# S4 block with adaLN and a Mish MLP: input transform behind each chunk on TensorE, VectorE's small work dealt out, parameters of blocks 1 and 2 at the start

## The chip, the cores and the metric

One core of a Trainium2 chip runs the whole program in one launch. The metric is device time in microseconds, the median of three runs. Five engines work from queues of their own: TensorE (PE, its weight loads shown as PEld), VectorE (DVE), ScalarE (ACT), GpSimd (POOL) and SyncE (SP), which here issues nearly all DMAs.

## The reference

A sequence of 2048 rows of 512 features goes through a state-space convolution and a two-layer MLP, each behind a layer norm whose scale, shift and gate come from a conditioning vector:

```python
mod = (_silu(c) @ w_mod).reshape(1, 6, 1, -1)      # sa, ca, ga, sb, cb, gb
h = _layernorm(x) * (1 + ca) + sa
x = x + ga * ssm(h)                                # below
h = _layernorm(x) * (1 + cb) + sb
x = x + gb * (mish(h @ w1 + b1) @ w2)              # 512 -> 1792 -> 512

# ssm: each of 512 features has 128 complex states (A, B, C) and a step dt
P = exp(dt * A * arange(2048))                     # (512, 128, 2048)
K = sum_n(C_n * P_n * dt * B_n).real               # a filter of 2048 taps for each feature
y = irfft(rfft(K, 4096) * rfft(h, 4096))[:2048] + h * Dskip
```

All arrays are float32.

## The kernel before

It has three stages. The **generation stage** (to about 319 us) makes the filters `K` of all features and takes them, and the normalized input, through the first step of a Fourier transform. The **product stage** finishes both transforms, multiplies them and transforms back. The **dense stage** is the MLP. Only the first is touched.

*Blocks and chunks.* The 512 features are four blocks of 128; a block is eight chunks of 16 features, so there are 32 chunks, `k` = 0 to 31. A power P over 2048 steps is put together from a coarse and a fine part, so for each chunk:

- `s_ang` (TensorE): two groups of four matmuls turn the block's phases into angles, into `pang`. `s_sin` (ScalarE): absolute value and two sines of these into `ec`, three instructions. It runs two chunks ahead; `ec` has three buffers, and the one for chunk k + 2 is free when TensorE has read that of chunk k - 1.
- `coarse` (TensorE, then ScalarE): magnitudes by a matmul into `pco` and an Exp into `co`. This is made for a whole block in one go, the **visit** before the block's first chunk: 16 matmuls and 16 Exps through two PSUM buffers, between two ScalarE table loads (the Exp and the sine do not share a table).
- `s_mag` and `s_comb` (VectorE): `m` from `co` (one product of 1024 elements for each partition), then four products of `ec` with `m` and `co`, of 1024, 512, 512 and 1024. Before, `m` has one buffer and is made at the end of the chunk in front.
- `s_kgen` (TensorE): 32 small matmuls of `ec` with itself give the filter in `pkg`; `s_ks` (ScalarE) copies it to `ks`, `s_skip` (VectorE) adds the skip term, `s_ka` (TensorE) takes it through the first Fourier step into `pka`, and `s_tm` (ScalarE) copies that to `gk`.

*Parameters.* `params(b, stage)` turns a block's raw B, C and A into the numbers that the phases come from. Its 35 or so VectorE instructions of 128 or 256 elements for each partition are in stages 0, 2, 3 and 5; stage 1 (Ln and Exp) and stage 4 (Arctan) are ScalarE's. The result `pk` is stored to DRAM, and loaded back in another layout as `s` (the tiles s3 and s12). Before, block 0 is done at the start, stages 0 and 2 of block 1 too; the rest of blocks 1 to 3 is spread over chunks 1, 2, 4 and 5 of the blocks in front.

*Input.* The rows come in eight tiles `x` of two halves. `u_stats` (VectorE) makes mean and variance of two tiles, `u_norm` (VectorE, four instructions) normalizes a tile with the gains, `u_mm` (TensorE) takes a half through its first Fourier step into `pua`, and `u_out` (ScalarE and a DMA) copies and stores it. The gains need the modulation: `mod_mm` (TensorE), `mod_out` (ScalarE, and a store to `md`), and `gains` loads that row back.

*What sets the order.* In the generation stage nothing is left to the scheduler: each instruction of VectorE, ScalarE and TensorE is chained to the one recorded before it on its engine. The order is that of the loop at line 561, which puts together a list for each chunk: first what the table `pe` has (the input's matmuls), then `s_ka`, `s_kgen`, `s_ang`, then ScalarE's parts with what `se` has, then `s_comb`, `s_skip` and what `ve` has (normalization, statistics, parameters), then a visit where one is due, then `s_mag` of the next chunk:

```python
steps = pe.get(k, []) + [(s_ka, k - 3), (s_kgen, k - 1), (s_ang, k + 3)]
steps += [(s_tm, k - 3), (s_ks, k - 1)] + se.get(k, []) + [(s_sin, k + 2)]
steps += [(s_comb, k), (s_skip, k - 2)] + ve.get(k, [])
```

The visits have other work dealt into them, by the number of the Exp behind which it stands: both halves of an angle group, a filter, a Fourier step.

Of the kernel before, what the change touches and what calls it, by code (L numbers as in the profile page):

```python
# [10 lines left out]
F32 = mybir.dt.float32  # L11
# [5 lines left out]
OP = mybir.AluOpType  # L17
# [67 lines left out]
def s4_block(ctx, tc, io, out):  # L85
# [39 lines left out]
    V, A = Ordered(nc.vector, "dve"), Ordered(nc.scalar, "act")  # L125

# [93 lines left out]
    def params(b, stage):  # L220
        r = raw[b]
# [25 lines left out]
        if stage == 1:  # L247
            act(row[2], w2, AF.Ln)
            act(row[3], row[2], AF.Exp, scale=-0.5)
# [16 lines left out]
        if stage == 4:  # L266
            act(row[2], row[7], AF.Arctan)
# [10 lines left out]
        if stage == 5:  # L278
# [3 lines left out]
            split(0, 2 if b == 0 else 6)  # L282

    CO, S3 = {}, {}

    def load_s(b, eng):
        for h in range(2):
            eng.dma_start(S12[(2 * b + h) % 3][0:64].bitcast(F32),
                          view(pkd, (P * b + 64 * h) * 12 * P, [[3 * P, 64], [16 * 12 * P, 4], [1, 2 * P]]))

    def load_s3(b, eng):
        eng.dma_start(pkd[b], PKR[b].rearrange("p i e n -> p (i e n)").bitcast(F32))
        S3[b] = pre.tile([64, 8, P], F32R, tag="s3", name=f"s3_{b}")
        eng.dma_start(S3[b].bitcast(F32), view(pkd, P * b * 12 * P + 2 * P,
                                               [[3 * P, 64], [16 * 12 * P, 8], [1, P]]))
# [28 lines left out]
    def s_mag(k):  # L324
        m = M2[k] = gen.tile([P, 16, 64], F32, tag="m2", name=f"m2_{k}", bufs=1)
# [4 lines left out]
    def s_comb(k):  # L330
        ec, m = EC[k], M2[k]
        V.tensor_mul(ec[:, :, :, 32:64], ec[:, :, :, 95:63:-1], m[:, None, :, 0:32].to_broadcast([P, 2, 16, 32]))
        V.tensor_mul(ec[:, 0, :, 64:96], ec[:, 0, :, 64:96], m[:, :, 32:64])
        V.scalar_tensor_tensor(ec[:, 1, :, 64:96], ec[:, 1, :, 64:96], -1.0, m[:, :, 32:64],
                               op0=OP.mult, op1=OP.mult)
        V.tensor_mul(ec[:, :, :, 0:32], ec[:, :, :, 0:32], CO[k][:, None, :, 0:32].to_broadcast([P, 2, 16, 32]))
# [60 lines left out]
    def rsqrt(dst, var, n, pool, tag):  # L397
# [16 lines left out]
    def gains():  # L414
        g = conv.tile([P, 2, D], F32, name="gs")
# [5 lines left out]
        g12.append(g)  # L421

# [9 lines left out]
    def u_stats(n):  # L432
        s6 = conv.tile([P, 4, 6], F32, tag="bst", name="bst", bufs=2)
        for h in range(4):
            V.bn_stats(s6[:, h], XT[n + h // 2][:, h % 2])
            V.bn_aggr(mv[:, 2 * n + h, :], s6[:, h])
        rsqrt(rstd[:, 2 * n:2 * n + 4], mv[:, 2 * n:2 * n + 4, 1], 4, conv, "rsq")

    def u_norm(n):
        x = XT[n]  # L440
        for h in range(2):
            j = 2 * n + h
            V.scalar_tensor_tensor(x[:, h], x[:, h], mv[:, j, 0:1], g12[0][:, 1], op0=OP.subtract, op1=OP.mult)
# [379 lines left out]
```

## Time and profile before

| | us |
|---|---|
| median of 3 runs | 779.54 (778.78 to 780.31) |
| the profiled execution | 780.22 |
| its span | 778.4 |
| PE, DVE, ACT busy in the span | 667.6, 441.8, 316.0 |
| mean granted clock of PE | 0.898 of full speed |

The page divides the span in 40 slices of 19.5 us; each digit is a busy share in tenths (9 is 90% or more), PEclk the granted clock in tenths of 2.4 GHz:

```
PE   0498679866986899999993699999999999999996
DVE  8278998797879769487762922443244315242113
PEclk9959865896598779999995799999999999999999
```

The first 16 slices are the generation stage: there PE's clock is mixed and PE is busy for 4 to 9 tenths behind the first slice, VectorE for 2 to 9. From the 17th slice on PE is busy for nearly all of each slice at full clock, but for the change from the product to the dense stage at 410 to 439 us. A row of the trace gives, for each instruction or group, its start and duration, the engine, the line, the operation, what it writes and reads, and in brackets how long its engine was idle before it and whom it waited for.

### The profile page before, as it was taken

What the parts mean: (1) busy time and instruction counts of PE and PEld (TensorE: products, weight loads), DVE (VectorE), ACT (ScalarE), POOL (GpSimd) and SP (SyncE); (2) the same over time, 40 slices, a digit from 0 to 9 for tenths busy, and PEclk for the clock granted to TensorE, in tenths of its full rate; (3) what the DMA queues carried; (4) which work ended last, traced back from release to release, by engine and by line L of the source; (5) the groups of instructions that cost most, each with busy time, mean ns of one, the idle gap of its engine ahead of it and who ended that gap; (6) DMA issues with size and microseconds to landing.
All of it is one profiled execution on the core that took longest, in us unless ns stands there. A gap on an engine that the chain in (4) does not pass through costs nothing.

```text
span 778.4 us, 11803 instructions
## 1 busy us (share of the span) xinstructions
PE 667.6 (86%) x4848; PEld 448.3 (58%) x4848; DVE 441.8 (57%) x813; ACT 316.0 (41%) x466; POOL 5.0 (1%) x12
## 2 busy tenths in 40 slices
PE   0498679866986899999993699999999999999996
PEld 0256445543564565433330486888778877888885
DVE  8278998797879769487762922443244315242113
ACT  1456446664584686444430532232223221222220
POOL 2000000000000000000000000000000000000000
PEclk9959865896598779999995799999999999999999
DMA  6604201610151053799827652204220220002002
GB/s 183 228 1 144 80 31 56 210 56 28 55 164 55 29 189 110 207 287 294 281 98 182 194 123 55 54 1 109 54 55 1 47 62 1 0 7 49 0 1 54
DMA packets 34218, 74.56 MB, mean 96 GB/s; under 512 B 5322, under 2 KB 9806, under 8 KB 33652
## 3 DMA queue, kind: packets, MB, share of 16 engines
q1 hardware_dynamic: 33284, 72.17, 32.1%
q10 hardware_dynamic: 576, 1.05, 0.7%
q8 instruction: 38, 0.62, 0.3%
q0 software_dynamic: 304, 0.59, 0.3%
q14 instruction: 16, 0.13, 0.1%
HBM read 49.66 MB, written 24.13 MB: 95 GB/s over the span
## 4 chain that ended last, share of the span: by engine, by line
PE 74%; DVE 13%; ACT 6%; issue 3%; DMA 2%; SPq 0%; DVEq 0%; ACTq 0%
PE pm L712 20%; PE po L729 20%; PE pang L134 5%; PE pka L134 4%; PE pub L470 4%; PE pkg L134 4%; PE pz L632 4%; PE pkb L470 4%; DVE ec L119 3%; PE pco L134 3%; PE pua L134 3%; DVE raw L119 2%; PE pmod L134 2%; ACT ec L128 2%; PE pia L677 1%
## 5 line engine op out<-in xcount | busy, mean ns | idle before, releaser
L712 PE MATMUL pm<-hh,w1h 128*128 128x512 f32 x448 | 142.6, 398 | 0.6 <-ACT hh L119 0.6
L128 ACT ACTIVATE mh<-pm,b 128x512 f32<-128x512 f32 x56 | 38.5, 688 | 228.1 <-PE pm L712 228.1
L119 DVE TENSOR_TENSOR mal<-mh,mah 128x512 fp32r<-128x512 f32 x56 | 38.7, 691 | 155.3 <-ACT mah L119 154.9
L712 PEld LDWEIGHTS pm<-hh,w1h 128*128 128x128 f32 x448 | 84.7, 189 | 21.7 <-ACT hh L119 1.6
L729 PE MATMUL po<-w2h,mah 128*128 128x512 f32 x224 | 89.4, 399 | 0.0
L712 PE MATMUL pm<-hh,w1l 128*128 128x512 f32 x224 | 88.7, 396 | 0.0
L729 PE MATMUL po<-w2l,mah 128*128 128x512 f32 x224 | 88.6, 395 | 0.0
L729 PE MATMUL po<-w2h,mal 128*128 128x512 f32 x224 | 88.5, 395 | 0.0
L134 PE MATMUL pang<-ac,s 96*128 96x512 f32 x128 | 56.8, 482 | 26.6 <-DMA s<-pkd 26.6
L119 DVE TENSOR_TENSOR ec<-ec,m 128x1024 f32<-128x1024 f32 x64 | 61.3, 958 | 12.0 <-ACT ec L128 7.4
L134 PE MATMUL pua<-x,da 64*128 64x512 f32 x64 | 30.9, 946 | 30.2 <-DVE x L119 23.4
L134 PEld LDWEIGHTS pka<-bdk,ks 128*64 128x64 f32 x512 | 35.1, 166 | 31.8 <-issue 24.3
L119 DVE TENSOR_TENSOR m<-co 128x1024 f32<-128x1024 f32 x32 | 39.0, 1219 | 23.7 <-ACT co L128 23.7
L134 PE MATMUL pka<-bdk,ks 128*64 128x128 f32 x512 | 44.0, 327 | 7.9 <-DVE ks L119 7.9
L729 PEld LDWEIGHTS po<-w2h,mah 128*128 128x128 f32 x224 | 42.1, 188 | 14.6 <-ACT mah L119 4.9
L119 DVE TENSOR_TENSOR y<-pkb,f 128x1024 f32<-128x1024 f32 x32 | 37.7, 1219 | 22.6 <-PE pkb L470 16.7
L134 PEld LDWEIGHTS pang<-ac,s 96*128 96x128 f32 x128 | 28.2, 220 | 37.0 <-issue 30.6
L712 PEld LDWEIGHTS pm<-hh,w1l 128*128 128x128 f32 x224 | 42.4, 189 | 10.0
L729 PEld LDWEIGHTS po<-w2h,mal 128*128 128x128 f32 x224 | 42.1, 188 | 10.2
L729 PEld LDWEIGHTS po<-w2l,mah 128*128 128x128 f32 x224 | 42.1, 188 | 9.8
L134 PE MATMUL pco<-mc,s 64*128 64x384 f32 x64 | 32.4, 586 | 17.6 <-ACT co L128 17.6
L134 PE MATMUL pang<-am,s 96*128 96x512 f32 x128 | 44.8, 436 | 0.0
(96 smaller groups left out, 914.0 us busy)
## 6 DMA issues: line engine op xcount, KB each, us to landing
ud<-u SPq DMA_DIRECT2D x16, 512.0 KB, 2.9
ur<-ud SPq DMA_DIRECT2D x32, 256.0 KB, 5.2
zd<-z SPq DMA_DIRECT2D x16, 512.0 KB, 3.0
zl<-zd SPq DMA_DIRECT2D x28, 256.0 KB, 4.9
x<-in_A_u SPq DMA_DIRECT2D x32, 128.0 KB, 3.0
x<-in_A_u SPq DMA_DIRECT2D x8, 512.0 KB, 7.2
out<-ot SPq DMA_DIRECT2D x32, 128.0 KB, 2.4
w1s<-in_B_w SPq DMA_DIRECT2D x8, 448.0 KB, 6.4
```

The costliest lines, as they stand in the source:

```text
L119: ins = getattr(self.engine, name)(*a, **kw)
L128: follow("act", nc.scalar.activation(out, in_, f, **kw))
L134: follow("pe", T.matmul(out, lhsT, rhs, start=start, stop=stop))
L470: T.matmul(p[64 * r:64 * r + 64, c, :], MQ["mf", q // 4][:, 2 * (q % 4) + r, 64 * c:64 * c + 64], rhs(r), start=True, stop=True)
L632: T.matmul(p[:, r, :], mi[64 * r:64 * r + 64, q % 4, c, :], Y[q][64 * r:64 * r + 64, c, :], start=(c == 0), stop=(c == 1))
L677: T.matmul(p[64 * tl:64 * tl + 64, :], di, ZL[tt, hv][:, j % 2, tl, :], start=True, stop=True)
L712: T.matmul(p, w1[wi][:, k, fs], hh[:, hi, k, :], start=(n == 0), stop=(n == 3 * KB - 1))
L729: T.matmul(PO[tt][q], a[ai][:, P * q:P * q + P], w2[wi][:, f, :], start=(f == 0 and n == 0), stop=(f == FB - 1 and n == 2))
```

## The change

Five things change, all in the generation stage.

1. *Order on TensorE.* In a chunk the filter and the angles come first, then the Fourier step of the filter, and the input's matmuls (`u_mm`) last; their output copies (`u_out`) move one chunk later.
2. *Order on VectorE.* The small functions no longer issue their instructions; they return lists (class `Later`). The loop deals a chunk's small instructions out between the chunk's own large products. `m` of the next chunk stands behind the first product of `ec`, and has two buffers.
3. *Normalizations* are put at other chunks, three of them (table `vt`) at the end of chunks 7, 15 and 23, in front of a visit.
4. *Parameters.* Blocks 1 and 2 are computed together, instruction by instruction in turn, at the start, between block 0's and the first sines, and stored there; block 3's stay in the loop, at chunks 2, 5, 8 and 10.
5. *Visits* are bare: only the 16 matmuls and Exps (visit 0 has the products of chunk 0 and `m` of chunk 1 on VectorE). The angles of chunk 2 come after visit 0.

The core of the diff:

```diff
+    class Later:
+        def add(self, f, *a, **kw):
+            self.ops.append(lambda: f(*a, **kw))
+        def __getattr__(self, name):
+            return lambda *a, **kw: self.add(getattr(V, name), *a, **kw)
...
     def load_params(b):
-        raw[b] = gen.tile([P, 16, P], F32, tag="raw" if b else "ec", name=f"raw{b}", bufs=1 if b else 3)
-        (load if b < 2 else nc.sync.dma_start)(raw[b][:, 0:6, :], io["par"][b].rearrange("p (k n) -> p k n", k=6))
+        raw[b] = gen.tile([P, 16, P], F32, tag="raw" if b % 2 else "ec", name=f"raw{b}", bufs=1 if b % 2 else 3)
+        load(raw[b][:, 0:6, :], io["par"][b].rearrange("p (k n) -> p k n", k=6))
...
     def s_mag(k):
-        m = M2[k] = gen.tile([P, 16, 64], F32, tag="m2", name=f"m2_{k}", bufs=1)
+        m = M2[k] = gen.tile([P, 16, 64], F32, tag="m2", name=f"m2_{k}", bufs=2)
...
+    def run(*lists):
+        for i in range(max(map(len, lists))):
+            for ops in lists:
+                if i < len(ops):
+                    ops[i]()
...
+    store_pk(0)
+    load_s(0)
+    load_params(2)
...
-    params(1, 0)
+    V.on = A.on = True
+    run(params(1, 0), params(2, 0))
+    tables("natural_log_exp_and_others")
+    run(params(1, 1), params(2, 1))
+    tables("trig_and_small")
+    run(u_stats(0), params(1, 2), params(2, 2))
+    run(params(1, 3), params(2, 3))
+    run(params(1, 4), params(2, 4))
+    run(params(1, 5))
+    store_pk(1)
+    load_params(3)
...
-    visit(0, {2: [(s_mag, 0), (s_comb, 0), (s_ang, 2, 0)], 4: [(s_ang, 2, 1), (s_mag, 1)], 9: [(s_kgen, 0)]})
+    run(params(2, 5))
+    visit(0, {2: [lambda: step(s_mag, 0), lambda: run(comb(0))], 4: [lambda: step(s_mag, 1)]})
+    store_pk(2)
+    s_ang(2)
...
-    for n, k in enumerate((4, 6, 8, 10, 14, 16, 20, 24)):
+    for n, k, d in ((0, 4, ve), (1, 7, vt), (2, 9, ve), (3, 12, ve), (4, 15, vt), (5, 17, ve), (6, 20, ve), (7, 23, vt)):
...
-            at(pe, k + 1 + s, u_mm, n, s)
-            at(se, k + 1 + s, u_out, n, s)
+            t = k + 1 + s
+            at(pe, t, u_mm, n, s)
+            at(se, t + 1, u_out, n, s)
...
-        steps = pe.get(k, []) + [(s_ka, k - 3), (s_kgen, k - 1), (s_ang, k + 3)]
-        steps += [(s_tm, k - 3), (s_ks, k - 1)] + se.get(k, []) + [(s_sin, k + 2)]
-        steps += [(s_comb, k), (s_skip, k - 2)] + ve.get(k, [])
+        for s in [(s_kgen, k - 1), (s_ang, k + 3), (s_ka, k - 3)] + pe.get(k, []):
+            step(*s)
+        for s in [(s_ks, k - 1)] + se.get(k, []) + [(s_sin, k + 2), (s_tm, k - 3)]:
+            step(*s)
+        own = comb(k) if 0 < k < NG else []
+        if k % 8 != 7:
+            own.insert(1, lambda: step(s_mag, k + 1))
+        own.append(lambda: step(s_skip, k - 2))
+        extra = [o for f, *a in ve.get(k, []) for o in f(*a)]
+        for i, o in enumerate(own):
+            o()
+            for e in extra[len(extra) * i // len(own):len(extra) * (i + 1) // len(own)]:
+                e()
+        for f, *a in vt.get(k, []):
+            run(f(*a) or [])
         if k % 8 == 7 and k + 1 < NG:
-            steps += [(visit, k // 8 + 1, {3: [(s_ang, k + 4, 0)], 5: [(s_ang, k + 4, 1)], 9: [(s_kgen, k)],
-                                           10: [(s_ks, k)], 11: [(s_ka, k - 2)], 12: [(s_tm, k - 2)]})]
-        steps += [(s_mag, k + 1)]
+            visit(k // 8 + 1)
+            step(s_mag, k + 1)
```

How the order moves is shown at three places. On ScalarE at the start, before, behind the arctangent of block 0 (`raw0`) come the first sines (`ec0`):

```order
L128 ACTIVATE raw0_81<-raw0_81 128x128
L119 ACTIVATE ec0_263<-pang0_245 128x2x16x32
L128 ACTIVATE ec0_263<-pang0_245 128x2x16x32
L128 ACTIVATE ec0_263<-ec0_263,halfpi_100 128x2x16x32
L119 ACTIVATE ec1_267<-pang1_254 128x2x16x32
```

and now, with `raw1` and `raw2` the parameters of blocks 1 and 2:

```order
L141 ACTIVATE raw0_81<-raw0_81 128x128
L144 ACT_TABLE_LOAD
L141 ACTIVATE raw1_152<-raw1_152 128x128
L141 ACTIVATE raw2_197<-raw2_197 128x128
L141 ACTIVATE raw1_152<-raw1_152 128x128
L141 ACTIVATE raw2_197<-raw2_197 128x128
L144 ACT_TABLE_LOAD
L141 ACTIVATE raw1_152<-raw1_152 128x128
L141 ACTIVATE raw2_197<-raw2_197 128x128
L119 ACTIVATE ec0_337<-pang0_319 128x2x16x32
```

Two table loads and six instructions on parameters, which wait for VectorE's, now stand ahead of the first sines.

On VectorE in chunk 4, before, with `x0` the first input tile, `gs` the gains and `m2_5` the next chunk's `m` (the rows between the products and `x0` are parameters of block 2):

```order
L119 TENSOR_TENSOR m2_4_594<-co4_325 128x1024
L119 TENSOR_TENSOR ec4_499<-ec4_499,m2_4_594 128x32x32
L119 TENSOR_TENSOR ec4_499<-ec4_499,m2_4_594 128x16x32
L119 SCALAR_TENSOR_TENSOR ec4_499<-ec4_499,m2_4_594 128x16x32
L119 TENSOR_TENSOR ec4_499<-ec4_499,co4_325 128x32x32
L119 TENSOR_TENSOR ks2_577<-ks2_577,dtap_86 128x4
...
L119 SCALAR_TENSOR_TENSOR x0_199<-x0_199,mv_134,gs_588 128x512
L119 SCALAR_TENSOR_TENSOR x0_199<-x0_199,rstd_135,gs_588 128x512
L119 SCALAR_TENSOR_TENSOR x0_199<-x0_199,mv_134,gs_588 128x512
L119 SCALAR_TENSOR_TENSOR x0_199<-x0_199,rstd_135,gs_588 128x512
L119 TENSOR_TENSOR m2_5_671<-co5_365 128x1024
```

and now:

```order
L119 TENSOR_TENSOR ec4_559<-ec4_559,m2_4_642 128x32x32
L119 TENSOR_TENSOR m2_5_709<-co5_396 128x1024
L119 SCALAR_TENSOR_TENSOR x0_201<-x0_201,mv_134,gs_637 128x512
L119 TENSOR_TENSOR ec4_559<-ec4_559,m2_4_642 128x16x32
L119 SCALAR_TENSOR_TENSOR x0_201<-x0_201,mv_134,gs_637 128x512
L119 SCALAR_TENSOR_TENSOR ec4_559<-ec4_559,m2_4_642 128x16x32
L119 TENSOR_TENSOR ec4_559<-ec4_559,co4_389 128x32x32
L119 SCALAR_TENSOR_TENSOR x0_201<-x0_201,rstd_135,gs_637 128x512
L119 TENSOR_TENSOR ks2_629<-ks2_629,dtap_86 128x4
L119 SCALAR_TENSOR_TENSOR x0_201<-x0_201,rstd_135,gs_637 128x512
```

`m` of the next chunk and the four instructions on the input tile moved from behind the products to between them; the parameters of block 2 are gone from here.

On TensorE in the chunk that first has input matmuls, before:

```order
L134 MATMUL pua000_673<-x0_199,da_103 128x512
L134 MATMUL pua001_674<-x0_199,da_103 128x512
L134 MATMUL pka2_677<-bdk_102,ks2_577 64x32x4 x8
L134 MATMUL pkg4_686<-ec4_499 32x64 x32
L134 MATMUL pang8_719<-ac_88,s12_2_96 128x512
```

and now:

```order
L147 MATMUL pkg4_719<-ec4_559 32x64 x32
L147 MATMUL pang8_752<-ac_88,s12_2_96 128x512
...
L147 MATMUL pka2_761<-bdk_102,ks2_629 64x32x4 x8
L147 MATMUL pua000_770<-x0_201,da_103 128x512
L147 MATMUL pua001_771<-x0_201,da_103 128x512
```

The filter of chunk 4 and the angles of chunk 8 no longer stand behind the matmuls that wait for the normalized tile.

## Rows read from the trace of the kernel before

**Rows 1.** Timeline, VectorE: start, duration, group, then idle time before and its releaser.
```profile
38.51 1.23 DVE L119 TENSOR_TENSOR m<-co 128x1024 f32<-128x1024 f32 x1 [14.59 <-ACT co L128]
...
73.38 0.69 DVE L119 SCALAR_TENSOR_TENSOR gs<-gs,ga 128x512 f32<-128x512 f32 x1 [1.09 <-DMA ga<-md]
...
310.60 0.16 DVE L119 TENSOR_TENSOR ks<-ks,dtap 128x4 f32<-128x4 f32 x1
```

**Rows 2.** Busy time by stretch: PE, PEld, DVE, ACT, POOL, then PEclk, DMA share, GB/s.
```profile
38.50:311.00 272.50, 221.01 (x2780) 143.89 (x2780) 225.24 (x379) 167.21 (x261) 0.00 (x0) 0.77 0.27 86
```

**Rows 3.** The chain that ended last, in order of time: start, duration, what.
```profile
52.34 3.71 PE pang L134 x8
...
88.63 1.99 PE pang L134 x8
...
91.69 1.02 PE pka L134 x16
92.71 1.13 PE pkg L134 x60
...
319.15 1.94 PE pub L470 x8
```

**Rows 4.** Timeline, VectorE: a chunk with nothing else in it, and statistics of two tiles.
```profile
152.20 1.22 DVE L119 TENSOR_TENSOR m<-co 128x1024 f32<-128x1024 f32 x1
153.55 1.96 DVE L119 TENSOR_TENSOR ec<-ec,m 128x1024 f32<-128x1024 f32 x2
155.42 0.69 DVE L119 SCALAR_TENSOR_TENSOR ec<-ec,m 128x512 f32<-128x512 f32 x1
156.02 1.22 DVE L119 TENSOR_TENSOR ec<-ec,co 128x1024 f32<-128x1024 f32 x1
...
157.23 2.07 DVE L119 TENSOR_TENSOR raw<-raw 128x256 f32<-128x256 f32 x6
...
166.61 0.69 DVE L119 BATCH_NORM_STATS2 bst<-x 128x6 f32<-128x512 f32 x1
...
172.22 1.22 DVE L119 TENSOR_TENSOR m<-co 128x1024 f32<-128x1024 f32 x1
```

**Rows 5.** Waits of VectorE, 26 to 318 us: total, times, longest.
```profile
DVE m L119 <- ACT co L128: 23.7, 4, 14.6
DVE raw L119 <- ACT raw L128: 20.5, 6, 4.9
DVE ec L119 <- ACT ec L128: 7.4, 5, 6.0
```

**Rows 6.** Busy time of tile `raw` (DVE, ACT), then of `pk` (DVE), chunks 1 to 9.
```profile
39.00:150.00 111.00, 19.16 (x58) 1.85 (x6) 0.72 0.24 79
...
39.00:150.00 111.00, 3.82 (x4) 0.72 0.24 79
```

**Rows 7.** Timeline, SyncE's DMA issues.
```profile
21.27 1.95 SPq L137 DMA_DIRECT2D s<-pkd  x3
...
63.88 0.78 SPq L383 DMA_DIRECT2D md<-mrow  x1
```

**Rows 8.** DMA issues to 90 us: count, KB each, us from issue to landing.
```profile
raw<-in_par SPq DMA_DIRECT2D x3, 384.0 KB, 5.0
...
ga<-md SPq DMA_DIRECT2D x1, 256.0 KB, 5.2
```

**Rows 9.** Timeline, ScalarE: the first sines and Exps, and Exps of a later visit.
```profile
30.40 1.02 ACT L119 ACTIVATE ec<-pang 128x1024 f32<-128x1024 f32 x1 [15.85 <-PE pang L134]
...
36.32 1.28 ACT L131 ACT_TABLE_LOAD   x1
37.61 0.87 ACT L128 ACTIVATE co<-pco 128x384 f32<-128x384 f32 x2
...
118.39 0.87 ACT L128 ACTIVATE co<-pco 128x384 f32<-128x384 f32 x2 [0.40 <-PE pco L134]
```

**Rows 10.** Groups by line: VectorE's normalization, count, busy us, mean ns.
```profile
L119 DVE SCALAR_TENSOR_TENSOR x<-x,mv,gs 128x512 f32<-128x512 f32 x16 | 11.9, 745 | 0.0
```

More of the change, by code (lines that the diff above doesn't have):

```diff
@@ L247, in params @@
         if stage == 1:
-            act(row[2], w2, AF.Ln)
-            act(row[3], row[2], AF.Exp, scale=-0.5)
+            V.add(act, row[2], w2, AF.Ln)
+            V.add(act, row[3], row[2], AF.Exp, scale=-0.5)
         if stage == 3:
@@ L266, in params @@
         if stage == 4:
-            act(row[2], row[7], AF.Arctan)
+            V.add(act, row[2], row[7], AF.Arctan)
         if stage == 2:
@@ L282, in params @@
             split(0, 2 if b == 0 else 6)
+        return V.ops
     CO, S3 = {}, {}
[L286 to L295, printed above, removed]
     def coarse(k, h):
@@ L471, in transform @@
                          start=True, stop=True)
+    def run(*lists):
[3 more added lines that the diff above has]
+                    ops[i]()
     tables("natural_log_exp_and_others")
     act(sc, cT, AF.Exp, scale=-1.0)
[L476 to L477 removed]
+    run(params(0, 0))
+    run(params(0, 1))
     V.tensor_scalar(sc, sc, 1.0, None, op0=OP.add)
@@ L486, in s4_block, with store_pk, load_s @@
     load(ident, io["ident"])
-    params(0, 3)
+    run(params(0, 3))
     tables("trig_and_small")
-    params(0, 4)
-    params(0, 2)
-    params(0, 5)
-    class SP:
-        dma_start = staticmethod(load)
-    load_s3(0, SP)
-    load_s(0, SP)
+    run(params(0, 4))
+    run(params(0, 2))
+    run(params(0, 5))
+    def store_pk(b):
+        load(pkd[b], PKR[b].rearrange("p i e n -> p (i e n)").bitcast(F32))
+    def load_s(b):
+        S3[b] = pre.tile([64, 8, P], F32R, tag="s3", name=f"s3_{b}")
+        load(S3[b].bitcast(F32), view(pkd, P * b * 12 * P + 2 * P, [[3 * P, 64], [16 * 12 * P, 8], [1, P]]))
+        for h in range(2):
+            load(S12[(2 * b + h) % 3][0:64].bitcast(F32),
+                 view(pkd, (P * b + 64 * h) * 12 * P, [[3 * P, 64], [16 * 12 * P, 4], [1, 2 * P]]))
+    store_pk(0)
+    load_s(0)
+    load_params(2)
     for k in range(0, KB, 2):
@@ L514, in step, with visit @@
         f(*a)
-    def visit(b, others):
+    def visit(b, others={}):
         tables("natural_log_exp_and_others")
@@ L519, in visit @@
             coarse(8 * b + i // 2, i % 2)
-            for s in others.get(i, []):
-                step(*s)
-        if b + 1 < NB:
-            params(b + 1, 1)
+            run(others.get(i, []))
+        if b == 1:
+            run(params(3, 1))
         tables("trig_and_small")
-    u_stats(0)
     s_ang(0)
     s_ang(1)
-    V.on = A.on = True
     s_sin(0)
     s_sin(1)
-    params(1, 2)
-    visit(0, {2: [(s_mag, 0), (s_comb, 0), (s_ang, 2, 0)], 4: [(s_ang, 2, 1), (s_mag, 1)], 9: [(s_kgen, 0)]})
-    pe, se, ve = {}, {}, {}
+    run(params(2, 5))
+    visit(0, {2: [lambda: step(s_mag, 0), lambda: run(comb(0))], 4: [lambda: step(s_mag, 1)]})
+    store_pk(2)
+    s_ang(2)
+    pe, se, ve, vt = {}, {}, {}, {}
     def at(d, k, f, *a):
@@ L573, in s4_block @@
-        steps += [(s_mag, k + 1)]
-        for i, s in enumerate(steps):
-            tc.cur_priority = 100000 + int(10000 * (k + i / len(steps)))
-            step(*s)
+        tc.cur_priority = 100000 + 10000 * k
+        for s in [(s_kgen, k - 1), (s_ang, k + 3), (s_ka, k - 3)] + pe.get(k, []):
[5 more added lines that the diff above has]
+            own.insert(1, lambda: step(s_mag, k + 1))
```

74 lines of the change are left out of this document (43 added, 31 removed).

## Prediction

> **What bounds the kernel now.** Read the table by stages first, then the long VectorE stretch. The product and dense stages are not touched; what the change can move is the generation stage, from the first product on VectorE at 38.51 to the last one's end at 310.60 us [rows 1]. In that stretch of 272.1 us VectorE is busy 225 us, PE 221 us at a mean granted clock of 0.77, ScalarE 167 us [rows 2]. PE's figure is stretched by the clock: one chunk's three matmul groups (angles 1.99, filter 1.13, Fourier step 1.02 us) are 4.14 us at 2.4 GHz, while the same angles take 3.71 us at 1.2 GHz [rows 3]. VectorE needs 5.03 us for a chunk with nothing else in it: 152.20 to 157.23 [rows 4]. So VectorE is the slower of the two in every chunk, and it carries all the small work besides. Now its waits: 20.5 us for ScalarE's logarithm or arctangent of the parameters (six waits), 23.7 for `co` (14.59 of it before the first product), 7.4 for `ec` [rows 5, 1]. The stage is thus a VectorE queue: work plus these waits. I price it there and check PE and ScalarE afterwards.
>
> **What leaves the stretch 38.5 to 310.6.**
> 1. Parameters of blocks 1 and 2 leave it: 19.2 us of durations in 58 instructions on `raw` and 3.8 in 4 on `pk`, 23.0 together [rows 6]. An instruction of this kind starts up to 0.08 us before the one in front ends, and some follow their operand with a gap; from start to start I take 20 us (bounds 18 and 23).
> 2. The six waits for ScalarE go: 20.5 us [rows 5]. Those of blocks 1 and 2 go with the work. Block 3's also go, because its Ln stands in the visit before chunk 8 and its arctangent early in ScalarE's chunk 10, ahead of VectorE's use.
> 3. Order within a chunk. `m` of the next chunk now stands between the four products, in a second buffer. In the row, `ec` starts 1.35 us after an `m` of 1.22, but the independent 0.69 us product is followed after 0.60 [rows 4]: waiting for the result just written costs 0.13, not waiting gains 0.08, so 0.21 a chunk, 6.7 us over 32. VectorE's idle time is 272.5 - 225.2 = 47.3 us; the waits named above hold 37.0 of it, the gains' 1.1 [rows 1]; the 9.2 left are such gaps. Beyond the 0.13 x 32 of them I let 3 us of the small work's gaps go. Together 9.7 (bounds 0 and 13).
> 4. Old waits for `co` at the three later visits, 23.7 - 14.6 = 9.1, for `ec` 7.4, and for the gains 1.1: taken out here, 17.6, and set anew below.
>
> The Trainium skill speaks against step 3: "VectorE: DVE Perf Modes", § The DRAIN you can't avoid, says that each VectorE instruction waits until the pipe of the one before is empty and that a semaphore between them costs nothing extra. By it step 3 is worth 0 and the sum below is 9.7 us longer. The rows differ: 0.60 and 1.35 cannot both be explained by the duration alone.
>
> **What comes in.**
> 5. A later start. VectorE now begins the parameters of blocks 1 and 2 together, and its order is kept, so its first instruction on block 2 waits for a load that SP issues only behind the three loads of `s` (21.27 + 1.95 us; I take 1 us off, since block 1 no longer stands among block 0's work) [rows 7]. A parameter load lands 5.0 us after its issue [rows 8]: 27.3. VectorE was idle from 23.9 to 38.5 [rows 1], so that wait itself is free; what follows is not. Stages 0, 2 and 3 of two blocks are 62 instructions at 19.2/58 = 0.33 less 0.08 when two blocks alternate: 15.5; I take 14, as the long reciprocals and the gaps of dependent pairs weigh less here. The statistics of the first two tiles are dealt in there: 166.61 to 172.22, 5.6 us for the same work in one run [rows 4]; 5.3 here. VectorE reaches the arctangents at 46.6. ScalarE's order is kept too: two arctangents (0.6) stand ahead of the first two sine groups, which began at 30.40; `co` of chunk 0 began at 37.61, 7.2 us later (5.9 for two groups, 1.28 for the table), and the first `m` at 38.51 [rows 9, 1]. So 46.6 + 0.6 + 7.2 + 0.9 gives 55.3; I take the first product at 55.0, **16.5 us later** than before. Bounds: 10 (load lands early, no small gaps) and 22.
> 6. Visit 0 is now bare: 16 `co` at 1.27 us a pair (0.87 busy, 0.40 waiting for PE) [rows 9] = 10.2 us, to 64.3, and only then the angles of chunk 2 (3.71 at 1.2 GHz, 68.0) and its sines (2.9, 71). VectorE has done chunks 0 and 1 by 66.5: 4.5 us of waiting.
> 7. The gains. The modulation product stands behind chunk 2, 3 and 4's angles and the first filter; its row is copied at about 81.5. Before, from the issue of that store to the first use of the gains were 63.88 to 73.38, 9.5 us [rows 7, 1], with other issues between store and last load; the last load alone landed in 5.2 [rows 8]. With the three in one run I take 7.5: 89. VectorE arrives at 82, and the instruction now stands in the middle of chunk 3's products, so the filter of chunk 3 on PE and the sines behind it wait as well: 7 us (bounds 1 and 10). After this point VectorE is some 12 us behind the old schedule.
> 8. Visits 1 to 3. From the end of chunk 6 (14, 22): filter on PE 1.1, four copies of about 0.45 (an estimate, as for a `co`: 0.87 for two), sines 3.0, table 1.3, two `co` 0.9: 8.1, with hand-overs 8.3 us. VectorE has for it 5.03 - 1.35 = 3.7 us of products and a normalization, which the new table puts just there, 4 x (0.75 - 0.08) = 2.7 [rows 10]: 1.8 us of waiting each, 5.4 (4 each if PE is at 1.2 GHz). Then the sines needed two chunks later come only after the bare visit, at about 22.4, and for the next chunks behind PE's backlog. Visit 1 hides that (chunk 8 carries block 3's parameters and statistics, about 14 us in all); visit 2 shows 3, visit 3, with no small work behind it, 6: 9 us.
> 9. PE below full speed after VectorE's long chunks (7.7 us for a chunk with normalization against 4.14 of PE work) delays sines now and then: 3 us.
>
> **The sum.** 272.1 - 20 - 20.5 - 9.7 - 17.6 = 204.3; plus 4.5 + 7 + 5.4 + 9 + 3 = 28.9 gives 233.2. From 55.0 the last product ends at 288.2 instead of 310.6: 22.4 us earlier. The tail (last filter, Fourier step, modulation rows on PE) keeps its 8.5 us, 310.60 to the product stage's first matmul at 319.15 [rows 1, 3], and that stage follows rigidly, as its tables and `ur` loads are still issued during the last chunks. Check of the others: ScalarE's 167 us and PE's 221, even at its old clock, fit in 233. Moving the input matmuls behind the others gives nothing by itself: PE is not what ends the chunk; it only lets filter and sines go ahead of the wait for `x`. The profiled execution took 780.22 us (span 778.4), 0.68 over the median of 779.54. 780.2 - 22.4 - 0.7 = **757 us**.
>
> **Rivals.**
> A. *Everything fits better*: parameters ready at 49 instead of 55, gains wait 1 instead of 7: 12 us less, 745. For it: the load could land sooner, and PE may run at 2.4 GHz by the modulation. Against: both need luck at once.
> B. *PE becomes the bound.* A chunk at 1.2 GHz is 4.14 x 3.71/1.99 = 7.7 us against VectorE's 4.8. Some 15 chunks have no small work; if half of them run so, 7 x 2.9 = 20 us are lost: 777. For it: bare visits (0.40 of each 1.27 idle) and longer VectorE chunks leave PE gaps, and the old granted clock was 0.77 already. [...] The Trainium skill, "Perfetto Trace Analysis", § Optimization Strategy, advises to interleave stages with different limits; the change does the opposite in the visits (angles, filter and transform leave them), and no row of before shows a bare one.
> C. *Slower.* The place is the start: 16.5 + 4.5 + 7 us are lost by chunk 3 for certain. If from then on a chunk is set not by VectorE's queue but by the loop through PE, ScalarE and back, taking work from VectorE pays nothing: only the waits of step 2 for blocks 1 and 2 come back, four of the six, some 14 us, and 779.5 + 28 - 14 = 794. It decides where that loop (filter, copy, sines, and what stands ahead of them on each engine) takes longer than three VectorE chunks, 14.5 us.
> D. *Dealing out saves nothing* (step 3 at 0): 767.
> That the change does not do what it says: the order shows it does; what could fail is only the overlap in the start, which A and C price.
>
> **How the numbers follow.** Forecast 0.55 (its own range 748 to 764), A 0.12, D 0.08, B 0.15, C 0.10. Range 742 to 776: it leaves out C and the edges of A and B. A difference of 0.2% (1.6 us) is about what can be told from none. Faster: forecast, A, D and most of B, 0.86; within 0.2%: 0.03; slower: C and a worse B, 0.11.
>
> **What would show it.** First `m` at 55 (49 to 60); one stop of several microseconds at `gs`; no wait of VectorE for `raw` on ScalarE behind the start; plain chunks of 4.8 us from `ec` to `ec`; waits for `co` of 2 to 4 us at each visit; the last `ec` near 288 and the first `pub` near 297. The prediction is wrong if the first `m` comes after 62, if chunks without small work take over 6 us, or if PE is busy without a gap at 1.2 GHz through most of the blocks.

## The result and the profile after

The changed kernel takes **761.57 us** (760.93 to 762.60, four runs) against 779.16 for the kernel before on the same chip; the ratio is 0.9773, with an interval of 0.9756 to 0.9791. So 17.6 us are gained where 22.4 were forecast; the forecast was 757 us, in a range of 742 to 776. The profiled execution took 760.93 us, its span is 759.2.

The length of the stretch came out as summed: from the first `m` at 55.84 to the end of the last product at 288.7 it is 232.9 us, for 233.2 forecast. VectorE's timeline in the kernel after, columns as in [rows 1], answers to [rows 1, 5]:

```profile
28.46 2.98 DVE L119 TENSOR_TENSOR raw<-raw 128x256 f32<-128x256 f32 x11 [11.11 <-DMA raw<-in_par]
...
53.97 0.95 DVE L119 CAST pk<-raw 128x768 fp32r<-128x768 f32 x1 [2.97 <-DMA pkd<-pk]
...
55.84 1.22 DVE L119 TENSOR_TENSOR m<-co 128x1024 f32<-128x1024 f32 x1
...
69.87 1.23 DVE L119 TENSOR_TENSOR ec<-ec,m 128x1024 f32<-128x1024 f32 x1 [3.22 <-ACT ec L141]
...
83.97 0.69 DVE L119 SCALAR_TENSOR_TENSOR gs<-gs,ga 128x512 f32<-128x512 f32 x1 [4.28 <-DMA ga<-md]
...
122.96 0.29 DVE L119 TENSOR_TENSOR raw<-raw 128x128 f32<-128x128 f32 x1 [5.99 <-ACT raw L141]
...
287.47 1.22 DVE L119 TENSOR_TENSOR ec<-ec,co 128x1024 f32<-128x1024 f32 x1
```

The reader is to see the long wait for block 2's parameters at 28.46, the first `m` 17.3 us later than before, the gains' stop, and one wait that was not in the forecast: 5.99 us for a logarithm in chunk 8. The waits of VectorE over 25 to 310 us (total, times, longest) answer to [rows 5]:

```profile
DVE ec L119 <- ACT ec L141: 12.7, 6, 3.7
DVE raw L119 <- DMA raw<-in_par: 11.1, 1, 11.1
...
DVE m L119 <- ACT co L141: 7.3, 3, 4.7
...
DVE raw L119 <- ACT raw L141: 6.3, 2, 6.0
```

Busy time of the stretch, columns as in [rows 2], and under it PE's first matmul of the product stage, which answers to the last of [rows 3]:

```profile
55.80:288.70 232.90, 200.75 (x2774) 135.94 (x2775) 198.08 (x322) 165.03 (x254) 0.00 (x0) 0.83 0.28 92
```
```profile
298.40 1.94 PE L486 MATMUL pub<-ur,mf 128*64 128x512 f32 x8 [0.68 <-ACT gk L119]
```

VectorE stands idle for 34.8 us of the stretch; before it was 47.3. The last product ends 22.0 us earlier than before, for 22.4 forecast. `pub` comes 20.75 us earlier: the tail from the last product to `pub`, which was to keep its 8.5 us, takes 9.7. The span is 19.2 shorter, so another 1.5 us are lost behind `pub`. From the first `pub` to the end the kernels below take 459.2 to 461.1 us, the kernel before 459.3, the one after 460.8; I did not trace either loss to a cause, and the second may be scatter. The last 1.6 us lie between the profiled executions and the medians.

A chunk with nothing else in it, VectorE in the kernel after; it answers to [rows 4]:

```profile
274.88 1.22 DVE L119 TENSOR_TENSOR ec<-ec,m 128x1024 f32<-128x1024 f32 x1
276.01 1.22 DVE L119 TENSOR_TENSOR m<-co 128x1024 f32<-128x1024 f32 x1
277.14 0.69 DVE L119 TENSOR_TENSOR ec<-ec,m 128x512 f32<-128x512 f32 x1
277.75 0.69 DVE L119 SCALAR_TENSOR_TENSOR ec<-ec,m 128x512 f32<-128x512 f32 x1
278.35 1.22 DVE L119 TENSOR_TENSOR ec<-ec,co 128x1024 f32<-128x1024 f32 x1
279.48 0.16 DVE L119 TENSOR_TENSOR ks<-ks,dtap 128x4 f32<-128x4 f32 x1
279.55 1.22 DVE L119 TENSOR_TENSOR ec<-ec,m 128x1024 f32<-128x1024 f32 x1
```

From `ec` to `ec` it takes 4.67 us instead of 5.03: every product starts 0.08 to 0.09 us before the one in front ends.

### The profile page after: what moved, and what is told of

Its sections match the earlier page's. It is cut to its first block, busy times and chain, and to the rows that moved or that the text cites. A ratio compares the mean times of both kernels' runs of the same rounds, so it can differ in the third digit from the quotient of the medians.

```text
span 759.2 us, 11837 instructions
## 1 busy us (share of the span) xinstructions
PE 649.6 (86%) x4848; PEld 440.8 (58%) x4848; DVE 431.8 (57%) x813; ACT 318.7 (42%) x468; POOL 5.0 (1%) x12
## 4 chain that ended last, share of the span: by engine, by line
PE 71%; DVE 14%; DMA 6%; ACT 6%; issue 2%; SPq 1%; ACTq 0%; DVEq 0%
PE pm L759 21%; PE po L776 20%; PE pang L147 5%; DVE ec L119 4%; PE pz L679 4%; PE pub L486 4%; PE pkg L147 3%; PE pkb L486 3%; DVE raw L119 3%; PE pco L147 3%; PE pka L147 2%; PE pia L724 2%; ACT co L141 2%; PE pmod L147 2%; DVE m L119 2%
## 5 line engine op out<-in xcount | busy, mean ns | idle before, releaser
L759 PEld LDWEIGHTS pm<-hh,w1h 128*128 128x128 f32 x448 | 84.8, 189 | 21.6 <-ACT hh L119 1.5
L147 PE MATMUL pang<-ac,s 96*128 96x512 f32 x128 | 55.1, 476 | 26.3 <-DMA s<-pkd 26.3
L119 DVE TENSOR_TENSOR ec<-ec,m 128x1024 f32<-128x1024 f32 x64 | 61.1, 955 | 13.4 <-ACT ec L141 12.7
L147 PEld LDWEIGHTS pkg<-ec 128*32 128x32 f32 x2048 | 37.6, 120 | 38.4 <-issue 31.1
L147 PE MATMUL pkg<-ec 128*32 128x64 f32 x2048 | 42.5, 241 | 18.9 <-DVE ec L119 5.9
L147 PEld LDWEIGHTS pco<-mc,s 64*128 64x128 f32 x64 | 16.9, 269 | 50.1 <-ACT co L141 47.2
```

Of the source, the lines that this page charges most:

```text
L119: ins = getattr(self.engine, name)(*a, **kw)
L147: follow("pe", T.matmul(out, lhsT, rhs, start=start, stop=stop))
L759: T.matmul(p, w1[wi][:, k, fs], hh[:, hi, k, :], start=(n == 0), stop=(n == 3 * KB - 1))
```

## The experiments

My theory was that VectorE's queue (its work plus the waits I named) bounds the generation stage, so that each edit is worth what it takes out of that queue. The rivals: PE and ScalarE bound it, so that removed waits come back under other names; and the dealing saves nothing. Times are medians, each beside runs of the kernel before on its chip (780.0 to 780.8 us); the intervals are those of the ratio to it. Differences to the changed kernel, which was measured on another chip, are those of the medians; by the ratios they come out 0.4 to 1.7 us lower, and what is called a difference below is one by both.

**1. The two halves of the change.** Only the parameters moved (old loop and visits, new start); and only the order changed (parameters of blocks 1 to 3 where they were):

```
# parameters alone: the changed kernel with the loop of before (cut to its core)
-        for s in [(s_kgen, k - 1), (s_ang, k + 3), (s_ka, k - 3)] + pe.get(k, []):
+        for s in pe.get(k, []) + [(s_ka, k - 3), (s_kgen, k - 1), (s_ang, k + 3)]:
-        if k % 8 != 7:
-            own.insert(1, lambda: step(s_mag, k + 1))
+        for o in own:
+            o()
+        for e in extra:
+            e()
...   (and: visits filled as before, step(s_mag, k + 1) behind the chunk, u_norm at its old chunks)

# order alone: the changed kernel with the parameters where they were (cut to its core)
-    run(params(1, 0), params(2, 0))
-    tables("natural_log_exp_and_others")
-    run(params(1, 1), params(2, 1))
+    run(params(1, 0))
+        at(ve, 8 * b + 1, params, b + 1, 3)
+        at(se, 8 * b + 2, lambda b=b: run(params(b + 1, 4)))
+        at(ve, 8 * b + 2, params, b + 1, 5)
```

> Only the parameters are moved: the prologue makes blocks 0, 1 and 2 as in the changed kernel, and the loop keeps its old order (m behind the products in one buffer, small work behind the products, old order on PE and ScalarE, visits filled with angles, filter and Fourier step, normalizations at their old chunks). Theory by steps 1, 2 and 5: 780 less 20 of work, less 13.5 for the four waits of blocks 1 and 2, plus 17.3 of later start, plus 3 for the gains: 767, 764 to 770. Rival (the old visits are what costs, with the late logarithm of block 3 behind a filled visit, 13 us of wait): 773 to 778.

> Only the order is new: bare visits, small work dealt out between the products, m in two buffers, input transform behind the others on PE; the parameters of blocks 1 and 2 are made where the kernel before makes them. Theory from the runs so far (filling the visits costs 12 us, dealing the small work out costs some 8, moving m is worth nothing): 780 less 12 plus 8, 774 to 778, and VectorE's waits for raw from ScalarE stay at 20 us or more. Rival (steps 3 and 4 as predicted, the order is worth its 9.7 and the old waits): 764 to 770.

The parameters alone: 784.20 us, ratio 1.0058 (1.0036 to 1.0079), slower by 0.6%. The order alone: **752.58**, ratio 0.9638 (0.961 to 0.9666), faster than both together: with the new order in place, too, the moved parameters cost time, 9 us. Both theories and both rivals were wrong here. VectorE's waits when only the parameters are moved:

```profile
DVE ec L119 <- ACT ec L141: 22.2, 5, 7.7
DVE m L119 <- ACT co L141: 11.7, 2, 6.1
...
DVE raw L119 <- ACT raw L141: 9.7, 3, 9.0
```

Against [rows 5], `raw` falls from 20.5 to 9.7, but `ec` rises from 7.4 to 22.2 and `co`, without the wait before the first product, from 9.1 to 11.7. Together they were 37.0 and are 43.6: the waits for the parameters of blocks 1 and 2 did not go, they became waits for the sines behind the same visits. Behind visit 2 it can be seen row by row, first in the kernel before, where VectorE waits for the logarithm and then for the arctangent, then with the parameters moved:

```profile
206.90 0.29 DVE L119 TENSOR_TENSOR raw<-raw 128x128 f32<-128x128 f32 x1 [2.64 <-ACT raw L128]
...
220.36 0.62 DVE L119 SCALAR_TENSOR_TENSOR raw<-raw 128x128 f32<-128x128 f32 x2 [4.44 <-ACT raw L128]
```
```profile
218.18 1.95 DVE L119 TENSOR_TENSOR ec<-ec,m 128x1024 f32<-128x1024 f32 x2 [7.69 <-ACT ec L141]
...
225.03 1.95 DVE L119 TENSOR_TENSOR ec<-ec,m 128x1024 f32<-128x1024 f32 x2 [1.95 <-ACT ec L141]
```

The first `m` is at 55.45, the first `pub` at 319.39, 0.24 us later than before. With the order alone the list of waits reads:

```profile
DVE m L119 <- ACT co L141: 19.9, 4, 14.7
...
DVE raw L119 <- ACT raw L141: 9.9, 4, 6.4
DVE ec L119 <- ACT ec L141: 7.5, 4, 3.7
```

Here `raw` is down by half with the parameters still in the loop. What took those waits away is in the order. What went are the waits for the logarithms, the TENSOR_TENSOR rows on `raw`: 9.4 us in three before, 0.17 now. The waits for the arctangents, the SCALAR_TENSOR_TENSOR rows, were 11.1 us and are 9.7: 6.42 at 61.21, and

```profile
126.45 0.29 DVE L119 SCALAR_TENSOR_TENSOR raw<-raw 128x128 f32<-128x128 f32 x1 [0.80 <-ACT raw L141]
...
191.02 0.29 DVE L119 SCALAR_TENSOR_TENSOR raw<-raw 128x128 f32<-128x128 f32 x1 [2.52 <-ACT raw L141]
```

**2. The visits.** One edit to the kernel before, and its mirror to the changed one:

```
# bare visits in the kernel before
-            steps += [(visit, k // 8 + 1, {3: [(s_ang, k + 4, 0)], 5: [(s_ang, k + 4, 1)], 9: [(s_kgen, k)],
-                                           10: [(s_ks, k)], 11: [(s_ka, k - 2)], 12: [(s_tm, k - 2)]})]
+            steps += [(visit, k // 8 + 1, {})]
# filled visits in the changed kernel
-            visit(k // 8 + 1)
+            visit(k // 8 + 1, {3: [lambda: step(s_ang, k + 4, 0)], 5: [lambda: step(s_ang, k + 4, 1)],
+                               9: [lambda: step(s_kgen, k)], 10: [lambda: step(s_ks, k)],
+                               11: [lambda: step(s_ka, k - 2)], 12: [lambda: step(s_tm, k - 2)]})
```

> One edit to the kernel before: its visits 1 to 3 lose the angles, filter, copies and Fourier step that stood between their products; these follow behind the visit. Theory (the bare visit is what the gain comes from: it is some 7 us shorter on ScalarE, so the logarithms behind it and the sines of the next chunks come that much earlier): 780.4 less about 12, 766 to 771; VectorE's waits for raw and ec, 27.9 us together, fall by 6 or more. Rival (bare visits pay only with the new order of the chunks): 776 to 782.

> Visits 1 to 3 get back what the kernel before had between their products on PE: the two halves of the angles, the filter, its copies and the Fourier step of the neighbouring chunks. Theory (the bare visits delay the sines of the chunks behind them): the waits of VectorE for ec behind visits 1 to 3 (2.12 at 203.16, 2.59 at 255.43, 3.69 at 264.99 us, 8.4 together) shrink by 4 to 8 us, the waits for co do not grow since only co of later pairs come later: 754 to 758. Rival 1 (the loss moves into the visit: each co pair waits behind the angles, VectorE's m waits, 7.3 us now, grow by as much): 760 to 763. Rival 2 (PE's clock is what the filled visits keep): the granted clock over 100 to 290 us rises clearly and the time falls by more than 8 us, under 753.

Bare visits in the kernel before: 768.50 us, 0.9843 (0.9814 to 0.9872), as expected. Filled visits in the changed kernel: 773.81, 0.9909 (0.9887 to 0.9931), 12 us slower, where I had expected 4 to 8 faster; that came before the other run and turned my theory round. ScalarE in visit 1, in three kernels: the one before, the one before with bare visits, and the changed one with filled visits:

```profile
108.75 1.28 ACT L131 ACT_TABLE_LOAD   x1
...
127.29 1.28 ACT L131 ACT_TABLE_LOAD   x1
```
```profile
108.34 1.28 ACT L131 ACT_TABLE_LOAD   x1
...
112.17 0.87 ACT L128 ACTIVATE co<-pco 128x384 f32<-128x384 f32 x2 [0.40 <-PE pco L134]
...
119.27 0.64 ACT L128 ACTIVATE raw<-raw 128x128 f32<-128x128 f32 x2
119.93 1.28 ACT L131 ACT_TABLE_LOAD   x1
```
```profile
112.13 1.28 ACT L144 ACT_TABLE_LOAD   x1
...
117.69 0.87 ACT L141 ACTIVATE co<-pco 128x384 f32<-128x384 f32 x2 [2.13 <-PE pco L147]
120.63 0.87 ACT L141 ACTIVATE co<-pco 128x384 f32<-128x384 f32 x2 [2.07 <-PE pco L147]
...
130.14 0.64 ACT L141 ACTIVATE raw<-raw 128x128 f32<-128x128 f32 x2
130.80 1.28 ACT L144 ACT_TABLE_LOAD   x1
```

From table to table a bare visit takes 11.6 us, a filled one 18.5 and 18.7; the pair of Exps that took 1.27 us takes 2.9 where angles stand on PE between the products. Between the tables ScalarE can make no sine, and the logarithms stand at the visit's end. So with a filled visit VectorE's instruction on `raw` in chunk 8 waits 13.07 us instead of 5.99, and behind visits 2 and 3 it waits 6.79 and 8.83 for `ec`. In the kernel before, the bare visits bring `raw` from 20.5 to 8.3 and `ec` from 7.4 to 2.6 us. PE's granted clock over the stretch is higher with bare visits as well, 0.80 against 0.77 in the kernel before and 0.83 against 0.79 in the changed one; how much of the 12 us comes by way of the clock these runs do not separate. "Perfetto Trace Analysis" of the Trainium skill, § Optimization Strategy, holds that interleaving stages with different limits may help. In these visits the opposite was measured, the 12 us: what was put between the Exps held up ScalarE, for which the chunks behind wait.

**3. Order within a chunk (step 3).** `m` put back behind the products in one buffer; or the small work issued behind the products of its chunk; or PE's and ScalarE's old order:

```
# m back
-        m = M2[k] = gen.tile([P, 16, 64], F32, tag="m2", name=f"m2_{k}", bufs=2)
+        m = M2[k] = gen.tile([P, 16, 64], F32, tag="m2", name=f"m2_{k}", bufs=1)
-        if k % 8 != 7:
-            own.insert(1, lambda: step(s_mag, k + 1))
-            step(s_mag, k + 1)                   # behind a visit
+        step(s_mag, k + 1)                       # behind every chunk, and a visit
# not dealt out
-        for i, o in enumerate(own):
+        for o in own:
             o()
-            for e in extra[len(extra) * i // len(own):len(extra) * (i + 1) // len(own)]:
-                e()
+        for e in extra:
+            e()
# old order on PE and ScalarE
-            at(se, t + 1, u_out, n, s)
+            at(se, t, u_out, n, s)
...
-        for s in [(s_kgen, k - 1), (s_ang, k + 3), (s_ka, k - 3)] + pe.get(k, []):
+        for s in pe.get(k, []) + [(s_ka, k - 3), (s_kgen, k - 1), (s_ang, k + 3)]:
-        for s in [(s_ks, k - 1)] + se.get(k, []) + [(s_sin, k + 2), (s_tm, k - 3)]:
+        for s in [(s_tm, k - 3), (s_ks, k - 1)] + se.get(k, []) + [(s_sin, k + 2)]:
```

> Undoes the other half of step 3: m of the next chunk stands behind the chunk's products again, in one buffer; the small work is still dealt out. Theory: a plain chunk goes back from 4.68 us to the 5.03 of the kernel before, 0.35 in each of the 28 chunks that m was moved in, so 7 to 10 us slower, 768 to 771. Rival (PE or the loop through ScalarE sets the chunk, VectorE's order does not): no change, 760 to 763, and the 0.35 shows up as longer waits of VectorE for ec in the changed kernel.

> Undoes the dealing of the small work alone: a chunk's normalization, statistics, modulation pieces and parameter pieces are issued behind its four products instead of between them; m of the next chunk stays between the products, in two buffers. Theory (VectorE's queue bounds the generation stage, step 3 of the prediction): the 3 us that I gave to the small work's gaps come back, 761.6 to about 764.6; the plain chunks, which have no small work, keep 4.68 us from ec to ec. Rival (the dealing saves nothing, or even costs, since a chunk's products end later and with them its filter and the next sines): no change or up to 3 us faster, 758.5 to 761.6, with fewer waits of VectorE for ec.

> PE and ScalarE get their old order within a chunk: input transform first, then Fourier step, filter, angles on PE, Fourier copy ahead of the others on ScalarE. VectorE's order is not touched. Theory (the prediction gave this edit nothing by itself): within 2 us of the changed kernel, 760 to 764, a VectorE wait or two for ec longer. Rival (it is the PE order that lets the sines be early, the loop PE, ScalarE, VectorE bounds): VectorE's waits for ec (12.7 us in 6 waits now) grow to 20 us and more, 768 or later.

`m` back: 761.03 us, 0.9752 (0.9727 to 0.9778), no change. Its plain chunk is 5.03 us again (271.08 to 276.11 in its trace), and 27 chunks had `m` between their products, so VectorE's products should take some 27 x 0.36 = 9.7 us longer (an estimate from the plain chunk). Its waits shrink by nearly as much: `ec` from 12.7 to 7.7, `co` from 7.3 to 3.2, 9.1 together:

```profile
DVE ec L119 <- ACT ec L141: 7.7, 5, 3.1
...
DVE m L119 <- ACT co L141: 3.2, 2, 2.7
```

Not dealing out: **753.09**, 0.965 (0.9631 to 0.9669), 8.5 us faster; the rival's direction, and more than it gave. (Of this the two profiled executions show 5.8 us in the span.) A chunk with a normalization takes 7.33 us (151.43 to 158.76) against 7.32 dealt out (154.20 to 161.52), so there the dealing saves nothing by itself. What it costs is the place of a waiting instruction. VectorE in chunk 8 without the dealing, and under it the start of chunk 9 in the changed kernel:

```profile
114.94 1.23 DVE L119 TENSOR_TENSOR ec<-ec,m 128x1024 f32<-128x1024 f32 x1
116.08 1.22 DVE L119 TENSOR_TENSOR m<-co 128x1024 f32<-128x1024 f32 x1
...
122.84 0.29 DVE L119 TENSOR_TENSOR raw<-raw 128x128 f32<-128x128 f32 x1 [2.27 <-ACT raw L141]
...
131.64 1.22 DVE L119 TENSOR_TENSOR ec<-ec,m 128x1024 f32<-128x1024 f32 x1
```
```profile
134.97 1.22 DVE L119 TENSOR_TENSOR ec<-ec,m 128x1024 f32<-128x1024 f32 x1
```

The products are done before VectorE stops for the logarithm, the stop is 2.27 instead of 5.99 us, and chunk 9 starts at 131.64 instead of 134.97. The 1.52 us for `x` in the dealt order went too. Together these make 4.9 of the 5.8 us.

PE's old order: 764.00, 0.9792 (0.9772 to 0.9812), 2.4 us slower or nothing (the intervals overlap), near the forecast of none. VectorE's waits for `ec` are 12.2 us for 12.7, so the rival's growth did not come.

**4. Waits that were left.** The load of block 2's parameters moved ahead on SP; the logarithms at the start of visit 1; both with the undealt order; and with the gains one chunk later as well. In the order alone, the logarithms first and nothing dealt:

```
# load early
     load(ident, io["ident"])
+    load_params(2)
...
     load_s(0)
-    load_params(2)
# logarithms first (for the order alone: for b + 1 in each visit)
         tables("natural_log_exp_and_others")
+        if b == 1:
+            run(params(3, 1))
         for i in range(16):
             coarse(8 * b + i // 2, i % 2)
             run(others.get(i, []))
-        if b == 1:
-            run(params(3, 1))
# gains later
-    at(ve, 3, gains)
+    at(ve, 4, gains)
```

> The load of block 2's parameters is issued on SP right behind the load of the identity, ahead of block 0's store and of the three loads of s, instead of behind them. Theory (step 5: VectorE's start is late by this one load, since its first instruction on block 2 stands ahead of the work on block 1): the wait of 11.11 us before 28.46 shrinks to under 4 us, the arctangents come at about 37 to 39 instead of 46.4 and the first m at 46 to 49 instead of 55.84; everything behind follows, 752 to 755. Rival (the early load takes bandwidth from the store and the loads of block 0, whose s then sets the first sines): the first m comes at 52 or later and the time falls by less than 4 us, 758 to 762.

> In visit 1 the two logarithms of block 3's parameters stand ahead of the 16 copies co instead of behind them. Theory (step 2 missed this wait: VectorE's instruction on raw stands between the products of chunk 8 and waits for the last thing in the visit): the wait of 5.99 us before 122.96 goes, the first m of the visit comes 0.65 us later, and chunk 9 starts 4 to 5 us earlier than at 134.97; 756.5 to 758.5. Rival (the sines of chunk 9 could not be ready earlier, as they follow the visit on ScalarE): a wait of VectorE for ec of 3 us or more appears before chunk 9 and the time stays at 760 to 762.

> The changed kernel with three edits together: load of block 2's parameters early, logarithms of block 3 at the start of visit 1, small work behind the products. Theory (they remove different waits: 11.1 us at the start, 6.0 in chunk 8, and the dealing some 4 beyond the part of that same 6.0 that it shortened): 749.3 - 7.1 - 4.5 = 737.7, 735 to 741, with the last ec product at about 264. Rival (PE and ScalarE set the chunks once VectorE's waits are gone, so that waits for ec grow by as much): 745 to 750.

> As the run with the three edits together, and the gains one chunk later (chunk 4, ahead of the first normalization). Theory (step 7: the wait for the gains' load, 3 to 5 us before gs, is VectorE's own time): 3 to 4 us under the run with the three edits, no wait before gs left over 0.5 us. Rival (chunks 4 and 5 are bound by the sines, since the angles behind the modulation come late): no difference of more than 1 us, with a wait for ec of 2 us or more in chunks 4 to 6.

> The new order with the parameters of blocks 1 to 3 where the kernel before has them, and two more edits: small work behind the products of its chunk, and the logarithms at the start of each visit. Theory: the order alone took 752.6; no dealing is worth some 4 beside the shorter wait for the logarithm, the logarithms' place 1 to 3 (waits of 0.17, 0.80 and 2.52 us): 745 to 749. Rival (the small work of two blocks' parameters needs the dealing, or the waits return as ec): 751 to 755.

The early load: 749.25 us, 0.9594 (0.9567 to 0.9622), 12 less than the changed kernel and more than expected. SP issues it at 5.25 instead of 22.98, VectorE's wait of 11.1 us is gone, and the first `m` stands at

```profile
44.58 1.22 DVE L119 TENSOR_TENSOR m<-co 128x1024 f32<-128x1024 f32 x1
```

The logarithms first: 754.50, 0.9669 (0.9642 to 0.9696), 7 less. VectorE starts chunk 9 at 130.54 instead of 134.97 though its whole order began 0.42 us later, and after the first `m` stands for nothing in chunk 8:

```profile
115.08 1.23 DVE L119 TENSOR_TENSOR m<-co 128x1024 f32<-128x1024 f32 x1 [2.39 <-ACT co L141]
...
121.07 0.61 DVE L119 TENSOR_TENSOR raw<-raw 128x128 f32<-128x128 f32 x2
...
130.54 1.22 DVE L119 TENSOR_TENSOR ec<-ec,m 128x1024 f32<-128x1024 f32 x1
```

The three edits together: **738.87**, 0.9463 (0.944 to 0.9486), as summed. The gains later: 736.17, 0.9434 (0.941 to 0.9458), the fastest kernel here; the intervals of the two overlap, and though five of its six runs lie below all six of the other on the same chip, that last step alone is at most 2.7 us and not shown clear of noise. In its trace the wait of 2.13 us for the gains is gone, but the wait for `ec` at 183.70 is 3.46 where it was 2.28 without it:

```profile
183.70 1.23 DVE L119 TENSOR_TENSOR ec<-ec,m 128x1024 f32<-128x1024 f32 x1 [3.46 <-ACT ec L141]
```

The order alone with its two further edits: 753.79 (748.1 to 755.6), 0.9641 (0.9603 to 0.9679), no difference from 752.58. The expected 4 to 8 us did not come. The expectation had misread the waits of 0.80 and 2.52 us: they are for the arctangent, as the rows above show, and for the logarithms VectorE waited only 0.17, so their place had nothing to give. The waits for the arctangent did shrink, 9.7 to 3.5 us, with the small work behind the products, but the wait for `co` at visit 1 grew from 1.88 to 3.88, and without the dealing VectorE is busy 217.9 us in the stretch instead of 214.6. So leaving the dealing out paid only where a long wait stood between the products.

## Why the prediction was right in its number and partly wrong in its reasons

By its terms, the moved parameters were to give -20 - 20.5 + 16.5 + 7 = -17.0 us (steps 1, 2, 5, 7) and the order -9.7 - 17.6 + 4.5 + 14.4 + 3 = -5.4 (steps 3, 4, 6, 8, 9). Measured apart they are +3.8 and -27.9, together -17.6; the 6.5 us by which the two together give less than their sum I did not trace to a cause. Two errors of about 20 us cancelled in the sum, so the nearness of the number is in good part luck.

*Step 2 failed* (six waits for Ln and Arctan go with the parameters, 20.5 us). I took each wait by the name of its releaser. The logarithms stood last in a visit of 18.5 us, and the sines of the next chunks right behind it; without the `raw` instruction VectorE stops at `ec` a little later: waits of 37.0 us became 43.6. Behind them stood the length of the visit, and the bare visit is what removed much of it: in the kernel before, with nothing else changed, `raw` and `ec` fall from 27.9 to 10.9 us and the time by 12.3. It is a part of the change that step 8 entered only as new waits of 14.4. "Block 3's also go" was wrong too: the Ln stands at the end of visit 1, but VectorE's use of it between the products of chunk 8, as the 5.99 us show.

*Step 1* (20 us of work leave): the work left, and with the old order most of its time came, but no more than the later start took: the stretch is 16.7 us shorter (255.5 for 272.2, VectorE busy 21.6 less and idle 4.9 longer) and begins 16.9 later. Without the 20.5 of step 2 the terms for the moved parameters add up to +3.5, close to the +3.8 measured. With the new order less came: the stretch from first `m` to last `ec` is 229.2 us with the parameters moved (55.84 to 285.00) and 236.5 without (38.34 to 274.87), 7.4 less for a start 17.5 later. These stretches end at the first product of the last chunk. Up to the end of that chunk VectorE is busy 16.6 us less with the parameters moved (198.0 for 214.6) but idle 9.2 longer (34.8 for 25.6): the waits for sines grow from 7.5 to 12.7 and the one for the gains from nothing to 4.3. More than half of the work that left was replaced by waiting.

*Step 5* was right in size (55.84 for 55.0), with a wait of 2.97 us for the store of `pk` that I had not seen. But "that wait itself is free" was wrong: 11.3 us of the later start were this one load, which SP issued late, for the first `m` comes at 44.58 when it is issued early. With the early load the moved parameters are at best worth about 3 us (749.25 against 752.58 on the same chip, with overlapping intervals), without it they lose 9.

*Step 3*: the gain inside a chunk was larger than priced (0.36 for 0.21 us). The opening of "VectorE: DVE Perf Modes" in the Trainium skill, § The DRAIN you can't avoid, by which the next instruction starts only when the pipe is empty, does not fit the 4.67 us. The same paragraph adds that a next instruction that is not held starts earlier, so my reading of the page, by which step 3 is worth 0, was too strong. In the kernel's time the gain of `m` was worth nothing in this kernel: the waits took it back. Rival D (dealing saves nothing) was right on the dealing, which even lost 8.5 us here.

*Steps 6 to 9*: chunk 2's sines 3.22 for 4.5, the gains 4.28 for 7; the visits' waits for `co` 7.3 for 5.4 (1.86, 0.67 and 4.74, where 2 to 4 each was the sign), the waits for `ec` behind the later visits 9.5 for 9 (the 12.7 less the 3.22 of chunk 2). Together that is 24.3 for 25.9, near. Not in the sum were the 5.99 us for the logarithm and the 1.52 for `x`; the 3 us of step 9 can't be told apart in these rows.

*The tail* was to keep its 8.5 us and took 9.7.

Rival A did not come, nor did B and C as told: PE's granted clock rose from 0.77 to 0.83 of 2.4 GHz over the stretch, and bare visits, which I had put on B's side, paid. The 0.40 of each 1.27 us that B counts as idle is ScalarE's wait for PE, not a gap on PE. Half of C's idea, that VectorE's queue does not set all of the time, is what the runs show: with `m` back some 9.7 us of work came and the time stayed, and under the new order 16.6 us of parameter work left and 7.4 us of time came. That the loop through ScalarE sets it instead is argued from the names of the waits, `ec` and `co`, and not shown by itself.

Open: of the 27.9 us of the order, 12.3 are the bare visits; how the other 15.6 split over `m`, the dealing, PE's order and the new chunks of the normalizations was measured only from the changed kernel's side, where undoing `m` cost nothing, undoing the dealing gained 8.5 us and undoing PE's order cost 2.4 or nothing; the normalizations' chunks were not tried alone.

## What to carry to other kernels

An idle gap's releaser names what came last, not what the time hangs on: before booking a wait as saved, ask what the same engine would wait for next if that instruction were gone. A stretch in which an engine can't make what another needs (here ScalarE between two table loads) is to be kept short, even at the price of leaving it bare. In queues that run in order, an instruction that will wait long stands best behind the work that others need (8.5 us here, nothing in the kernel where those waits were short), and a load that the start waits for goes first on its issuing engine. And a change of several parts is to be measured in parts: here the whole was 9 us slower than one of its halves.

## What the hardware showed that I had not expected

Products of VectorE that don't use the result just written start 0.08 to 0.09 us before the one in front ends; 5.03 us of such work became 4.67 by order alone, more than the 0.21 that two rows of before had let me expect, because with `m` between them the first two products no longer stand back to back either: as a pair they take 1.96 us [rows 4], where their durations, 1.22 and 0.69, less such an overlap would be 1.83.
